# RetNet and quick-GELU on one core: v of steps 0 to 5 and q of step 3 loaded through GpSimd's DMA queue instead of SP's

## The chip, the cores and the metric

The kernel runs on one core of one Trainium2 chip. A core has five engines that work side by side, each through its own list of instructions in order: TensorE (PE) multiplies matrices, and its weight loads are counted apart (PEld); VectorE (DVE) and ScalarE (ACT) do elementwise work; GpSimd (POOL) does some of that and issues DMAs; SyncE (SP) issues DMAs alone. All DMAs, whoever issues them, are carried by the same 16 DMA engines. DMAs that SP or ACT issue appear in the profile as "hardware_dynamic" queues, those of GpSimd as "software_dynamic".

The metric is the device time of one execution in microseconds. An instruction waits for others by semaphores; a wait holds up everything behind it on the same engine, and that holds for DMA issues too.

## The reference: what is computed

Two blocks follow each other. The first is the RetNet recurrence for 4 batches, 8 heads, 768 positions and a head size of 64:

```python
gamma = 1.0 - 2.0 ** (-5.0 - np.arange(H))
for t in range(S):
    state = gamma * state + einsum('bhd,bhe->bhde', k[:, :, t], v[:, :, t])
    y[:, :, t] = scale * einsum('bhd,bhde->bhe', q[:, :, t], state)
```

Its output, regrouped to 3072 tokens of 512 numbers, goes through a feed-forward block with weights `w_in` (512 x 2048) and `w_out` (2048 x 512):

```python
h = x @ w_in
g = h * (1.0 / (1.0 + np.exp(-1.702 * h)))
return g @ w_out
```

The two weights arrive as 64-bit floats and are narrowed to 32 bits on the core.

## The kernel before

The recurrence is done in chunks of 64 positions. A step j handles one chunk of two batches; there are 24 steps, four steps make a block of 512 tokens, and six blocks go through the feed-forward part. While the first two blocks are computed, the kernel must also load and narrow the weights. This first stage, some 145 us, is written out by hand as one long list of names in the function's text (lines 998 to 1014): each engine carries out its own share of the list in that order, and so does each DMA queue.

The names that matter here, with j a step:

- `q{j}`, `k{j}`, `v{j}`: load the chunk of q, k or v (`load`, lines 131 to 170). For steps 0 to 5, q and k take four DMAs each and v two, all through `plain` and line 146, in pieces of 256 bytes; each of the three is 256 KB. q goes through SP; k through ACT for step 0 and through GpSimd for steps 1 to 5; v through SP. Buffers: q and v have two each, so v{j} has to wait until step j-2 has used its v, and q{j} until q{j-2} has been turned.
- `w{n}a`, `w{n}b`: fetch one half of a pair of weight columns, 512 KB (`fetch`, line 186), through SP, into one of three raw buffers; w3 needs the buffer that w0 leaves.
- `abs{n}` (ScalarE, L212), `half{n}` (VectorE, L216 to L218), `rest{n}` (VectorE, L222 to L227): narrow a weight. For w0 the two halves are done apart (0a, 0b).
- `turn{j}` (TensorE, L255): transpose k and then q of step j; `turned{j}` (ScalarE, L266) copies the results out of PSUM.
- `step{j}` (TensorE, L294): scores of q and k; `masked{j}` (VectorE, L323) masks them. `step-{j}` (L302, L311, L317): the products that read v and the masked scores; `step5-4` is step 5's scores followed by step 4's products. `updated{j}` (VectorE, L371, L373), `state{j}` (L330) and `x{j}` (L352) take their results, `aged{j}` (ScalarE, L362) scales the state by `whole`, and `decay{j}` (ScalarE, L277) scales k.
- `causal` (GpSimd, L919): cuts the mask, once VectorE has made it (`mask`, L954). `whole` (GpSimd, L930): loads a small table. `late` users of GpSimd in this stage are L940 to L948 (`anew`).
- `up0.h.n` (TensorE, L417): products of the feed-forward block 0 with weight n, each with a `gate` (ScalarE, L398).

One more order is imposed by the framework. Each kind of DMA queue has eight completion semaphores that its DMAs take in turn, SP and ACT sharing one set of eight, GpSimd having another. A DMA is issued only when the DMA eight places before it, which used the same semaphore, has landed.

Of the kernel before, what the change touches and what calls it, by code (L numbers as in the profile page):

```python
# [28 lines left out]
def kernel(  # L29
# [29 lines left out]
    pe, act, dve, pool, sp = nc.tensor, nc.scalar, nc.vector, nc.gpsimd, nc.sync  # L59
# [68 lines left out]
    NEW = 6  # L128
    QKV = {}

    def load(j, what="qkv"):

        b, c = j // NC * 2, j % NC
        rows = slice(c * D, (c + 1) * D)
        keep = tc.keep_in_program_order if j < 2 * CB else lambda i: i

        def plain(name, src, tag, bufs, engine=sp):
            t = two.tile([P, H, D], F32, name=name + "_in", tag=tag, bufs=bufs)  # L140
            QKV[name, j] = t
            for i in range(2):
                if j < NEW:
                    to, at = t[i * D:(i + 1) * D], src[b + i, :, rows, :].rearrange("h p d -> p h d")
                    for n in range(1 if name == "v" else 2):
                        keep(engine.dma_start(*((to, at) if name == "v" else (to[:, n:H:2], at[:, n * HP:(n + 1) * HP]))))  # L146
                else:
                    for r in range(2):
                        keep(engine.dma_start(t[r * D:(r + 1) * D, i * HP:(i + 1) * HP],
                                              src[b + i, r * HP:(r + 1) * HP, rows, :].rearrange("h p d -> p h d")))  # L150

        if j < NEW:
            if "q" in what:
                plain("q", q, "q_sq", 2)
            if "k" in what:
                plain("kn", k, "k_sq" if j in (0, 1, 4, 5) else "o", 2, pool if j else act)
        elif "q" in what:
            for name, src in (("q", q), ("k", k)):
                t = two.tile([P, H, D // C4, C4], F32, name=name + "_sq")
                for r0 in range(0, P, C4):  # L160
                    for n in range(D // C4):
                        t0 = c * D + n * C4
                        tc.keep_in_program_order((pool if (name, j) == ("k", 2 * CB - 1) else sp).dma_start(
                            t[r0:r0 + C4, :, n], src[b + r0 // D, :, t0:t0 + C4, r0 % D:r0 % D + C4]
                            .rearrange("h p d -> p h d")))
                QKV[name, j] = t
        if "v" in what:
            if j >= NEW and c < NC - 1:
                plain("kn", k, "kn", 1)
            plain("v", v, "v", 2)  # L170


    w1v = moe_w_in.bitcast(U32).rearrange("(c p) (f two) -> p c f two", p=P, two=2)
# [72 lines left out]
    def turn(j):  # L246

        QT[j], KT[j] = home(j, "qT"), home(j, "kT")
        if j < NEW:

            x = QKV.pop(("q", j)), QKV["kn", j]
            TURNED[j] = p = [ps.tile([P, HP, P], F32, name="pt", tag="y") for i in range(2)]
            for n in (1, 0) if j else (0, 1):
                for s in range(HP):
                    pe.matmul(p[n][:, s, :], x[n][:, 2 * s:2 * s + 2].rearrange("p r d -> p (r d)"), ident, is_transpose=True)  # L255
        else:
            for t, name in ((QT[j], "q"), (KT[j], "k")):
                tc.keep_in_program_order(dve.transpose(
                    t.rearrange("p h t -> p (h t)"), QKV.pop((name, j)).rearrange("p h n d -> p (h n d)")))
        if 2 * CB <= j < NCH - 2:  # L260
            load(j + 2, "qk")
# [113 lines left out]
    def step(j, f=None):  # L375
        attend(j, f)
        if j is not None:
            masked(j)
            if j > 2 * CB:
                decay(j)  # L380
        if f is not None:
            c = f % NC
            if c == 0:
                updated(f)
            else:
                by_state(f)
            output(f)
            if 0 < c < NC - 1:
                aged(f)
                updated(f)  # L390
        if j is not None and 2 * CB < j < NCH - 1:
            load(j + 1, "v")
# [541 lines left out]
    def late_loads():  # L934
        load(2 * CB, "qkv")
        load(2 * CB + 1, "qk")
# [174 lines left out]
```

## Time and profile before

| | us |
|---|---|
| median of 3 runs | 657.14 (656.97 to 660.35) |
| the profiled execution | 657.92 |
| its span | 656.2 |
| TensorE busy in the span | 638.8 (97%) |
| VectorE, GpSimd, ScalarE busy | 437.0, 188.4, 166.4 |
| TensorE busy in the first 60 us | 46.2 |
| data moved by DMA in the first 60 us | 203 GB/s on average |

The profile is one execution; its 657.92 us are 1.7 us more than its span, which runs from the first to the last instruction. Times given in the text as "at 8.47" are us from the start of that span. In a timeline each line has the start, the length, the engine, the line of the kernel, the operation, and out<-in with the count; a bracket at its end tells how long the engine had been idle before, and what ended that. A length beside a DMA issue is the time of issuing, not of the transfer; the trace tells apart when a transfer lands, engine by engine.

In the first 60 us TensorE is idle for 13.8 us, in the rest of the span for 3.6 us.

### The profile page before, as it was taken

What the parts mean: (1) busy time and instruction counts of PE and PEld (TensorE: products, weight loads), DVE (VectorE), ACT (ScalarE), POOL (GpSimd) and SP (SyncE); (2) the same over time, 40 slices, a digit from 0 to 9 for tenths busy, and PEclk for the clock granted to TensorE, in tenths of its full rate; (3) what the DMA queues carried; (4) which work ended last, traced back from release to release, by engine and by line L of the source; (5) the groups of instructions that cost most, each with busy time, mean ns of one, the idle gap of its engine ahead of it and who ended that gap; (6) DMA issues with size and microseconds to landing.
All of it is one profiled execution on the core that took longest, in us unless ns stands there. A gap on an engine that the chain in (4) does not pass through costs nothing.

```text
span 656.2 us, 15176 instructions
## 1 busy us (share of the span) xinstructions
PE 638.8 (97%) x6390; PEld 577.5 (88%) x6390; DVE 437.0 (67%) x609; ACT 166.4 (25%) x320; POOL 188.4 (29%) x218
## 2 busy tenths in 40 slices
PE   7689999999999999999999999999999999999997
PEld 3678888888888888889999888999888999888997
DVE  3789989999936963348885246987145986144854
ACT  4664234551000000333100323110333110332210
POOL 6400341310478218000627200535300334300000
PEclk9799999999999999999999999999999999999999
DMA  9995567853233455541577821477931254501142
GB/s 178 208 247 187 141 138 218 221 120 61 50 93 148 117 155 149 193 137 41 156 163 212 244 33 49 116 191 180 262 59 49 78 158 144 204 15 49 57 153 98
DMA packets 146229, 89.77 MB, mean 137 GB/s; under 512 B 129552, under 2 KB 132368, under 8 KB 145136
## 3 DMA queue, kind: packets, MB, share of 16 engines
q1 hardware_dynamic: 133680, 44.40, 29.8%
q0 software_dynamic: 9712, 38.43, 19.0%
q10 hardware_dynamic: 2768, 5.96, 2.6%
q8 instruction: 50, 0.82, 0.5%
q14 instruction: 19, 0.16, 0.1%
HBM read 71.32 MB, written 14.94 MB: 131 GB/s over the span
## 4 chain that ended last, share of the span: by engine, by line
PE 94%; DMA 2%; DVE 2%; SPq 1%; issue 0%; ACT 0%
PE pq L717 27%; PE px L590 17%; PE pd L852 15%; PE pz L590 8%; PE ph L417 8%; PE ph L488 6%; PE py L590 4%; PE pa L294 2%; DMA W<-in_moe_w_in_dram 2%; PE pa L302 2%; PE py L317 2%; PE py L311 2%; SPq L146 1%; PE pb L488 1%; PE pt L255 0%; DVE W L218 0%
## 5 line engine op out<-in xcount | busy, mean ns | idle before, releaser
L692 POOL DMA_DIRECT2D LATE<-W2D x28 | 15.5, 553 | 245.2 <-PE pq L717 123.8
L717 PE MATMUL pq<-W,G 128*128 128x128 f32 x672 | 80.2, 276 | 0.0
L717 PEld LDWEIGHTS pq<-W,G 128*128 128x128 f32 x672 | 77.6, 192 | 0.6
L590 PE MATMUL px<-X,W1A 128*128 128x256 f32 x256 | 60.5, 379 | 0.0
L590 PE MATMUL px<-X,LATE 128*128 128x256 f32 x256 | 60.5, 379 | 0.0
L717 PE MATMUL pq<-LATE 128*128 128x128 f32 x448 | 59.8, 276 | 0.0
L417 PE MATMUL ph<-X,W1A 128*128 128x256 f32 x256 | 57.4, 382 | 2.0 <-DVE X L352 1.1
L417 PEld LDWEIGHTS ph<-X,W1A 128*128 128x128 f32 x256 | 48.0, 190 | 9.0 <-DVE X L352 1.2
L717 PEld LDWEIGHTS pq<-LATE 128*128 128x128 f32 x448 | 54.5, 192 | 0.4
L590 PEld LDWEIGHTS px<-X,LATE 128*128 128x128 f32 x256 | 48.6, 190 | 6.6
L590 PEld LDWEIGHTS px<-X,W1A 128*128 128x128 f32 x256 | 48.4, 190 | 6.5
L852 PE MATMUL pd<-W,G 128*128 128x256 f32 x224 | 49.6, 381 | 0.0
L852 PEld LDWEIGHTS pd<-W,G 128*128 128x128 f32 x224 | 42.2, 190 | 5.9
L398 ACT ACTIVATE G<-G 128x512 f32<-128x512 f32 x49 | 30.8, 629 | 45.2 <-DVE G L645 19.7
L635 DVE TENSOR_TENSOR G<-pz,vv 128x512 f32<-128x512 f32 x16 | 11.1, 691 | 46.7 <-ACT vv L605 46.6
L852 PE MATMUL pd<-W,LATE 128*128 128x256 f32 x160 | 35.2, 380 | 0.0
L852 PEld LDWEIGHTS pd<-W,LATE 128*128 128x128 f32 x160 | 30.2, 190 | 4.3 <-DVE LATE L574 0.2
L739 ACT ACTIVATE o<-pq 128x512 f32<-128x512 f32 (+1 forms) x14 | 7.6, 544 | 90.7 <-PE pq L717 90.7
L590 PE MATMUL pz<-X,W1A 128*128 128x256 f32 x128 | 30.3, 379 | 0.0
L590 PE MATMUL py<-X,W1A 128*128 128x256 f32 x128 | 30.2, 379 | 0.0
L590 PE MATMUL pz<-X,LATE 128*128 128x256 f32 x128 | 30.2, 379 | 0.0
L717 PE MATMUL pq<-LATE,G 128*128 128x128 f32 x224 | 29.6, 275 | 0.0
(211 smaller groups left out, 1175.9 us busy)
## 6 DMA issues: line engine op xcount, KB each, us to landing
LATE<-W2D POOLq DMA_DIRECT2D x28, 768.0 KB, 4.9
W<-in_moe_w_in_dram SPq DMA_DIRECT2D x12, 512.0 KB, 5.9
W<-in_moe_w_out_dram SPq DMA_DIRECT2D x10, 512.0 KB, 6.1
out_dram<-o POOLq DMA_DIRECT2D x20, 256.0 KB, 4.0
q_sq<-in_q_dram SPq DMA_DIRECT2D x144, 32.0 KB, 2.2
v_in<-in_v_dram SPq DMA_DIRECT2D x72, 64.0 KB, 2.6
LATE<-W1D ACTq DMA_DIRECT2D x3, 1536.0 KB, 7.4
LATE<-W1D POOLq DMA_DIRECT2D x3, 1536.0 KB, 8.1
```

Source lines behind the costliest of these rows:

```text
L294: pe.matmul(pa[HALF[w], u, 0, s, :], kt[HALF[u], w, s, :], qt[HALF[u], w, s, :], start=True, stop=True)
L302: pe.matmul(pa[HALF[u], w, 1, s, :], kd[HALF[w], HP * u + s, :], vn[HALF[w], HP * u + s, :], start=True, stop=True)
L311: pe.matmul(py[HALF[o], u, 1, 2 * w + s2, :], old[HALF[u], w, 2 * s2 + o, :], qt[HALF[u], w, 2 * s2 + o, :], start=True, stop=True)
L317: pe.matmul(py[HALF[o], w, 0, 2 * u + s2 if f < NEW else 2 * s2 + u, :], vn[HALF[w], HP * u + s, :], a[HALF[w], u, s, :], start=True, stop ...
L398: pin(act.activation(g, h[:, i], AF.Gelu_apprx_sigmoid))
L417: pe.matmul(h[:, ab], w, X[:, 2 * th + c // 2, c % 2, :], start=(ab == 0 and c == 0), stop=(c == 3), skip_group_check=True)
L488: pe.matmul(acc[:, u, :], w, x, start=(start and u == 0 and c == 0), stop=(stop and c == 1), skip_group_check=True)
L590: pe.matmul(acc[:, u, :], w1(2 * d + u, sw)[:, c, :], X[:, sx, c, :], start=(start and u == 0 and c == 0), stop=(stop and c == 1), skip_gr ...
L635: dve.tensor_add(a[3], z, v)
L692: engine.dma_start(c, W2D[i])
L717: pe.matmul(p0[:, j, :], a[:, d], w[:, d], start=(new and j == 0 and d == 0), stop=(d == NP // 2 - 1), skip_group_check=True)
L852: pe.matmul(p0[:, n, :], g1(m, p, sa)[:, n * P:(n + 1) * P], W2[:, sb, p, :], start=(new and p == 0 and n == 0), stop=(last and p == NP - ...
```

## The change

`plain`, which issues the DMAs of one tile, takes the engine as an argument. The change passes GpSimd for v of steps 0 to 5 and for q of step 3:

```diff
         if j < NEW:
             if "q" in what:
-                plain("q", q, "q_sq", 2)
+                plain("q", q, "q_sq", 2, pool if j == 3 else sp)
             if "k" in what:
                 plain("kn", k, "k_sq" if j in (0, 1, 4, 5) else "o", 2, pool if j else act)
...
         if "v" in what:
             if j >= NEW and c < NC - 1:
                 plain("kn", k, "kn", 1)
-            plain("v", v, "v", 2)
+            plain("v", v, "v", 2, pool if j < NEW else sp)
```

The list of names stays as it is. TensorE, VectorE and ScalarE have the same instructions in the same order. On GpSimd the order in this stage becomes: small tables, k1, v0, k2, `causal`, v1, `whole`, k3, v2, q3, k4, v3, k5, v5, v4, then L940 and what follows. On SP it becomes: q0, w0b, q1, w0a, q2, w2b, w2a, q4, w3b, w3a, q5, w1b, w1a, w5b, w5a, w6. Sixteen DMAs change their queue, and with them the DMA eight places ahead for which each DMA waits.

## The prediction

> **What bounds the kernel now.** I read the page first, then the busy times by stage, the chain of waits, and the timelines of the queues and engines over the first 60 us.
>
> ```profile
> PE 638.8 (97%) x6390; PEld 577.5 (88%) x6390; DVE 437.0 (67%) x609; ACT 166.4 (25%) x320; POOL 188.4 (29%) x218
> ```
>
> TensorE sets the time: 656.2 - 638.8 = 17.4 us of the span is not TensorE work. By stage:
>
> ```profile
> 10.00:20.00 10.00, 6.72 (x107) 4.10 (x106) 6.67 (x11) 7.54 (x25) 6.52 (x10) 0.97 1.22 205
> 20.00:30.00 10.00, 7.79 (x176) 7.06 (x177) 7.22 (x12) 6.21 (x17) 4.25 (x7) 0.69 1.19 208
> 30.00:40.00 10.00, 9.34 (x168) 8.05 (x167) 7.25 (x10) 6.58 (x20) 0.00 (x0) 1.00 0.95 207
> 40.00:50.00 10.00, 7.78 (x130) 6.66 (x128) 9.79 (x13) 7.57 (x22) 0.00 (x0) 1.00 1.12 280
> ```
>
> The first figure after the length is TensorE's busy time, the last three are its granted clock, the DMA share and GB/s. 3.3, 2.2, 0.7 and 2.2 us of idle lie in these four rows, and from 60 us on TensorE is full. So this change, which ends before 50 us, can move only the first stage, and what it moves there is kept to the end. In that stage the DMA engines are full (shares near or over 1), which matters more than who issues. The chain of waits goes through them at w0a and again at w1:
>
> ```profile
> 8.47 9.20 DMA W<-in_moe_w_in_dram
> ...
> 36.45 4.00 DMA W<-in_moe_w_in_dram
> ```
>
> The SP queue, start and length of each group of issues:
>
> ```profile
> 7.13 1.30 SPq L146 DMA_DIRECT2D v_in<-in_v_dram  x2
> 8.47 1.08 SPq L186 DMA_DIRECT2D W<-in_moe_w_in_dram  x1
> 9.83 1.78 SPq L146 DMA_DIRECT2D v_in<-in_v_dram  x2
> 11.74 4.80 SPq L146 DMA_DIRECT2D q_in<-in_q_dram  x4
> 16.58 1.48 SPq L186 DMA_DIRECT2D G<-in_moe_w_in_dram  x2
> 18.17 1.95 SPq L146 DMA_DIRECT2D v_in<-in_v_dram  x2
> 20.16 9.04 SPq L146 DMA_DIRECT2D q_in<-in_q_dram  x8
> 29.30 1.96 SPq L186 DMA_DIRECT2D W<-in_moe_w_in_dram  x2
> ```
>
> These are v0, w0a, v1, q2, w2, v2, q3 with q4, w3. An undisturbed issue takes some 0.62 us; the long groups are SP held up. The weights w3 leave only behind q3 and q4. Then ScalarE, VectorE and GpSimd:
>
> ```profile
> 37.84 1.14 ACT L212 ACTIVATE W1A<-W 128x1024 f32<-128x1024 f32 x1 [3.42 <-DMA W<-in_moe_w_in_dram]
> ```
> ```profile
> 39.02 0.69 DVE L216 TENSOR_SCALAR W1A<-W1A 128x1024 f32<-128x1024 f32 x1 [2.35 <-ACT W1A L212]
> ...
> 47.13 0.68 DVE L216 TENSOR_SCALAR W1A<-W1A 128x1024 f32<-128x1024 f32 x1
> ```
> ```profile
> 12.82 1.84 POOL L919 TENSOR_SCALAR_AFFINE_SELECT mask<-mask 64x512 f32<-64x512 f32 x2 [4.08 <-DVE mask L954]
> 14.62 1.08 POOL L930 DMA_DIRECT2D whole<-in_col_decay_dram  x2
> ...
> 50.84 1.02 POOL L943 COPY cold<-cold 64x4 f32<-64x4 f32 x1 [24.12 <-ACT G L277]
> ```
>
> abs3 waits for w3 (3.42 us) and VectorE loses 2.35 us. GpSimd stands on a mask until 12.82 and is free from 26.7 to 50.8.
>
> **The change, part by part.** Sixteen DMAs (12 of v, 4 of q3) leave SP: 16 x 0.62 = 9.9 us of its issue time. The same sixteen come to GpSimd. Its k issues take 0.62 to 0.66 us, its shortest (row decay) 0.55, its longest (L467) 1.28; a v DMA has twice the pieces of a k DMA but nearest is k, so 0.67, and 16 x 0.67 = 10.7 us (8.8 to 20.5). The 24.1 us that GpSimd waits before L943 hide this; after it the last v leaves near 45, so 5 us of that cover stay, and if they went, the wait before L942 (16.2 us) would hide the rest. No instruction of PE, VectorE or ScalarE is added. What counts is when transfers land.
>
> *Price of a transfer.* In three rows the queues moved 205, 208 and 207 GB/s. Call the q, k or v of a step a tile (0.262 MB, 1.27 us at 207) and a half of w a block (0.524 MB, 2.53 us). Transfers of both queues land nearly in the order of issue: a 1 KB load (L930) issued at 15.15 took 5.3 us behind the others. From w0a's landing at 17.67, eight tiles and four blocks give 17.67 + 10.2 + 10.1 = 38.0 for w3; it landed at 37.76. A tile on GpSimd's queue may cost less (4 KB packets at 322 ns against sixteen of 29 ns: 0.87 of 1.27) or more (below): 0.9 to 1.8, and I take 1.27, which fits a mixed stage.
>
> *w0a, a gain.* It is issued at 7.13 instead of 8.47, and k2 (now behind v0 on GpSimd) falls behind it: it lands 1.27 us earlier, at 16.4. updated0 and step1 follow it: step1 at 19.85 instead of 21.13.
>
> *v1 and whole, a loss.* On GpSimd v1 stands behind the mask: 14.66 instead of 9.83. Without v, SP issues q2 and w2 from 8.6 to 12.5 (before, 11.74 to 18.1). So v1 lands behind k2, q2 and w2: 16.4 + 2.5 + 5.1 + 1.3 = 25.3 (18.7 before). step-1, which reads it, started at 24.09: +1.2 us, all of w0a's gain and as much again. whole, now behind v1, lands at 25.4 (20.4); aged1 (21.02) and turned2 (24.8) move to 25.4 and 27.8, in step with that.
>
> *q3, a loss.* Every DMA waits for the one eight before it on its kind of queue. v2 waits so for v1 (25), q3 for whole: q3 leaves at 26.0 to 28.5 instead of 20.16 to 25.5. SP meanwhile issues q4 (22.8, when turn2 is done) and w3 (25.4, 29.30 before). In order of landing: k3 26.5, q4 27.8, v2 29.1, w3 34.1, q3 35.4. turn3 read q3 at 32.42; it ends at 36.05 instead of 33.05: +3.0. step3 and masked3 follow through updated2 at +2.3.
>
> *w3, a gain that q3 eats.* w3 lands at 34.1 and abs3 no longer waits; the 2.35 us before half3 are gone. But masked3 stands ahead of half3 on VectorE and ends at 38.9: half3 starts at 38.95 against 39.02. Net -0.1.
>
> *q5 and w1, the next late thing.* q5 waits on SP for turn3 (36.05, before 33.20), and w1, w5 are queued behind it: w1 is issued at 38.7 and 39.3 (36.45, 37.89). After q3 come k4, v3, k5, q5, v5 and two blocks: 35.4 + 6.35 + 5.06 = 46.8 for w1 (42.43). abs1 then ends at 48.0 and half1, at 47.13 before, starts 0.9 late. rest1 and masked4 stand behind it on VectorE, and step5-4 on TensorE waits for masked4: +0.9.
>
> *The slowest engine.* A landing counts when the last of 16 DMA engines has finished. In the trace's landing records the last came 1.49 us after the fifteenth for w0a and 1.40 for w3a, while GpSimd's queue was active or just drained, and 0.01 for w1a. Now that queue is active until w1: I add 1.5 for w1, with 0 and 1.9 (w3b) as ends. The Trainium skill, DMA: Bandwidth & Descriptors, section Latency and other measured facts, says DMA engines 7 and 15 are usually slower, with fetches of GpSimd's descriptors as a best guess. The trace agrees on one late engine; it does not name it. If the guess held and each piece counted, the lag would double with the pieces; by the opposite reading it would be 0, and the sum 1.5 less.
>
> *v3, v4, v5, k4, k5.* k4 and k5 (needed at 39.4 and 43.4) and v3 (needed at 40.4) land at 36.7, 40.5 (its issue waits eight places, for q3) and 38.0: hidden by 2.4 us at the least; cover gone, each costs its lateness on TensorE. v4's buffer comes free with step-3 as before, and it has some 4 us until step5-4.
>
> Sum: w0a, v1, q3 and w3 together -0.1 at half3; w1 +0.9; slowest engine +1.5; step5-4's shift, +2.3. The clock was half from 19.4 to 26.3; a TensorE waiting until 25.3 may keep it so for one more 3.4 us window, 0 to 1.7 us; most lies under q3's wait, so I add 0.6. In all +2.9: 657.92 would become 660.8, and the median 657.14 becomes **660.0 us**.
>
> **The rivals.**
>
> *Faster: GpSimd's transfers need not queue behind the blocks.* For: k4's first part, issued at 18.13, landed at 25.86, before w2a (17.69, 26.77); a packet of 4 KB is cheaper. Against: L930's 5.3 us. If v1 takes 5.5 us it lands at 20.8, turn2 ends first (22.8), step-1 gains 1.3; q3 lands by 31, w3's 2.35 us are kept for the most part: -1.3 - 1.8 = -3.1, 654.0 us. It decides when v1 lands before 22.8 and q3 before 32.
>
> *A wash.* If the rate stays at 207 and one engine does not lag, w1's 0.9 and the clock are all that is left, or nothing where w3's gain is bigger: 657 us, -1.5 to +1.5. The Trainium skill, same page, section Issuing engines are not separate DMA queues, says that issuing from several engines saves only the sequencer's issue time. By that rule alone, with SP's issue off the end's path, this is the outcome; the rows above say that order of landing changes as well.
>
> *Slower by much.* The clock: v1 later than 25 leaves TensorE idle in the window to 26.3, then half-rate to 29.7 or 33.1. up0.0.0 (3.6 us at full rate) doubles and q3's lateness no longer covers it: +1.7 to 3.4 on my sum, 663 us.
>
> **How the numbers follow.** Forecast (+1 to +5): 0.42; faster rival (-1.5 to -4.5): 0.23; wash: 0.18; slow rival (+5 to +9): 0.17. 0.5% is 3.3 us, about what a measurement of this kernel can tell from no change: 653.9 and 660.4 are the bounds. Faster by over that: 0.16, of the faster rival. Slower: all of the slow rival and half of the forecast, 0.38. Within: 0.46. The range leaves out 0.1 at each end: 653.6 (w0a's, w3's gains whole) to 665.0 (bounds of lag and clock together). The forecast's own range is 658 to 662.
>
> **What would show it.** step1 near 19.9 (w0a right); step-1 near 25 with a wait on v_in; turn3 waiting for q_in near 35; no wait of abs3 on W; abs1 waiting for W near 46; TensorE idle before step5-4; a granted clock under 0.69 in 20 to 30. Wrong if v1 lands before 23, if q3 lands before 32, or if the 30 to 40 row moves well above 207 GB/s.

## The result and the profile after

The changed kernel takes 658.94 us (median of 22 executions, 657.67 to 662.96) against 656.96 us before: a ratio of 1.0028 with a 95% interval of 1.0017 to 1.0039, or +1.8 us (1.1 to 2.6; the two medians differ by 2.0). That is slower, by less than the 0.5% that a measurement was said to tell from no change. The forecast was 660.0 us, +2.9 us.

One thing has to be known before the traces are read. The profiled execution of the changed kernel (657.67 us) is the fastest of its 22, and that of the kernel before (657.92 us) lies 1 us above its own median. The two traces therefore differ by -0.25 us where the medians differ by +2.0, and they cannot show where the loss comes from. So both kernels were traced a second time (below: "second trace", 658.49 us after and 658.20 us before).

First the page's busy times, and the stages of the changed kernel from 10 to 50 us: after the length come the busy times of TensorE, its weight loads, VectorE, ScalarE and GpSimd, then TensorE's granted clock (the share of its full speed that it was allowed), the DMA share and GB/s.

```profile
PE 639.3 (97%) x6390; PEld 577.3 (88%) x6390; DVE 436.8 (67%) x609; ACT 166.5 (25%) x320; POOL 199.9 (30%) x234
```
```profile
10.00:20.00 10.00, 7.17 (x143) 4.45 (x143) 7.56 (x13) 8.04 (x25) 7.60 (x11) 1.00 1.13 248
20.00:30.00 10.00, 6.98 (x142) 5.76 (x141) 7.03 (x11) 6.31 (x20) 6.47 (x10) 0.71 0.91 210
30.00:40.00 10.00, 9.33 (x161) 7.92 (x161) 7.84 (x10) 5.88 (x17) 5.20 (x8) 0.94 0.71 152
40.00:50.00 10.00, 9.85 (x142) 8.59 (x141) 9.25 (x13) 8.36 (x25) 2.06 (x4) 1.00 1.05 312
```

GpSimd has 16 instructions and 11.5 us more; the busy times of the other engines differ by 0.5 us at most. Between 30 and 40 us the DMA share falls from 0.95 to 0.71, and from 207 to 152 GB/s. The second traces say the same (share 0.98 before, 0.79 after): with the change the DMA engines run out of issued work there. Part of the lower share has another reason. The moved tiles travel in packets of 4 KB, which took 292 and 314 ns on average in the two traces after, where the sixteen packets of 256 bytes that they replace took 28 to 29 ns each before. Over the first 60 us the same 203 to 204 GB/s need a DMA share of 0.83 and 0.87, against 0.95 and 0.96 before; the packets make 0.07 to 0.08 of that difference, an estimate from 448 and 7168 of them. The faster rival had named this in its favour, but the freed share was not turned into time.

The queues show why issued work runs out. SyncE, and then GpSimd, in the first trace after:

```profile
7.14 0.60 SPq L186 DMA_DIRECT2D W<-in_moe_w_in_dram  x1
7.96 3.00 SPq L146 DMA_DIRECT2D q_in<-in_q_dram  x4
11.00 1.13 SPq L186 DMA_DIRECT2D G<-in_moe_w_in_dram  x2
20.72 2.91 SPq L146 DMA_DIRECT2D q_in<-in_q_dram  x4
23.67 1.11 SPq L186 DMA_DIRECT2D W<-in_moe_w_in_dram  x2
34.49 3.08 SPq L146 DMA_DIRECT2D q_in<-in_q_dram  x4
37.61 1.13 SPq L186 DMA_DIRECT2D W<-in_moe_w_in_dram  x2
```
```profile
14.49 1.38 POOL L146 DMA_DIRECT2D v_in<-in_v_dram  x2
15.86 1.28 POOL L930 DMA_DIRECT2D whole<-in_col_decay_dram  x2
17.13 2.48 POOL L146 DMA_DIRECT2D kn_in<-in_k_dram  x4
22.49 0.69 POOL L146 DMA_DIRECT2D v_in<-in_v_dram  x1 [2.88 <-DMA v_in<-in_v_dram]
23.41 0.68 POOL L146 DMA_DIRECT2D v_in<-in_v_dram  x1 [0.23 <-DMA G<-in_moe_w_in_dram]
24.09 2.45 POOL L146 DMA_DIRECT2D q_in<-in_q_dram  x4
```

SP (w0a, q2, w2, q4, w3, q5, w1) now stands empty from 12.1 to 20.7 us, where q4 waits for turn2 to free its buffer, and from 24.8 to 34.5 us, where q5 waits for turn3. GpSimd issues v1 at 14.49, behind the mask, and v2 only after 2.88 us of waiting for v1's landing, the DMA eight places ahead of it; in the second trace it waits 4.72 us. q3 stands behind v2.

The waits on TensorE, in the second trace after (step1, step-1, up0.0.0, turn3, step5-4):

```profile
20.47 0.95 PE L294 MATMUL pa<-G 64*64 64x64 f32 x32 [3.17 <-DVE state L371]
...
24.40 1.55 PE L302 MATMUL pa<-v_in,G 64*64 64x64 f32 x30 [1.08 <-DMA v_in<-in_v_dram]
...
29.25 3.72 PE L417 MATMUL ph<-X,W1A 128*128 128x256 f32 x16 [0.79 <-DVE X L352]
...
35.56 0.63 PE L255 MATMUL pt<-UB,q_in 128*128 128x128 f32 x4 [2.15 <-DMA q_in<-in_q_dram]
...
54.72 0.69 PE L294 MATMUL pa<-G 64*64 64x64 f32 x32 [1.19 <-ACT W1A L212]
```

and the same places in the second trace before (step-1 without a wait):

```profile
20.74 0.69 PE L294 MATMUL pa<-G 64*64 64x64 f32 x32 [3.44 <-DVE state L371]
...
22.80 1.13 PE L302 MATMUL pa<-v_in,G 64*64 64x64 f32 x32
...
31.70 0.63 PE L255 MATMUL pt<-UB,q_in 128*128 128x128 f32 x4 [0.45 <-DMA q_in<-in_q_dram]
...
52.26 0.69 PE L294 MATMUL pa<-G 64*64 64x64 f32 x32 [0.91 <-DVE G L323]
```

Two waits for DMAs, on v1 (1.08 us) and on q3 (2.15 us), are there as forecast. From one second trace to the other step-1 comes later by 1.6 us, turn3's q part by 3.9 us and step5-4 by 2.5 us. The bracket of step5-4 after names L212, the abs of w5; but in all four traces step5-4 starts 0.15 us after masked4 has ended, and before the change that was ahead of the end of this abs. So it is masked4 that releases it. In the chain of waits of the first trace after, v1 and the last quarter of q3 have taken the place of w0a and w1:

```profile
14.49 7.45 DMA v_in<-in_v_dram
...
25.93 7.67 DMA q_in<-in_q_dram
```

### The profile page after: what moved, and what is told of

It is laid out like the page before. It is cut to its first block, busy times and chain, and to the rows that moved or that the text cites. A ratio compares the mean times of both kernels' runs of the same rounds, so it can differ in the third digit from the quotient of the medians.

```text
span 655.9 us, 15180 instructions
## 1 busy us (share of the span) xinstructions
PE 639.3 (97%) x6390; PEld 577.3 (88%) x6390; DVE 436.8 (67%) x609; ACT 166.5 (25%) x320; POOL 199.9 (30%) x234
## 4 chain that ended last, share of the span: by engine, by line
PE 93%; DMA 3%; POOL 1%; DVE 1%; issue 1%; ACT 0%; POOLq 0%
PE pq L717 27%; PE px L590 17%; PE pd L852 15%; PE pz L590 8%; PE ph L417 8%; PE ph L488 6%; PE py L590 4%; PE pa L294 2%; DMA v_in<-in_v_dram 2%; PE py L317 2%; PE py L311 1%; PE pa L302 1%; DMA q_in<-in_q_dram 1%; PE pb L488 1%; POOL kn_in L146 0%
## 5 line engine op out<-in xcount | busy, mean ns | idle before, releaser
L417 PE MATMUL ph<-X,W1A 128*128 128x256 f32 x256 | 59.4, 391 | 0.1
L417 PEld LDWEIGHTS ph<-X,W1A 128*128 128x128 f32 x256 | 49.4, 195 | 7.7 <-DVE W1A L227 0.4
L852 PEld LDWEIGHTS pd<-W,G 128*128 128x128 f32 x224 | 42.2, 190 | 5.9
L635 DVE TENSOR_TENSOR G<-pz,vv 128x512 f32<-128x512 f32 x16 | 11.1, 692 | 46.6 <-ACT vv L605 46.6
L717 PE MATMUL pq<-W,LATE 128*128 128x128 f32 x224 | 29.7, 275 | 0.5 <-issue 0.5
```

The costliest lines, as they stand in the source:

```text
L417: pe.matmul(h[:, ab], w, X[:, 2 * th + c // 2, c % 2, :], start=(ab == 0 and c == 0), stop=(c == 3), skip_group_check=True)
L635: dve.tensor_add(a[3], z, v)
L717: pe.matmul(p0[:, j, :], a[:, d], w[:, d], start=(new and j == 0 and d == 0), stop=(d == NP // 2 - 1), skip_group_check=True)
L852: pe.matmul(p0[:, n, :], g1(m, p, sa)[:, n * P:(n + 1) * P], W2[:, sb, p, :], start=(new and p == 0 and n == 0), stop=(last and p == NP - ...
```

## One gate: the start of half3

What a delay in this stage is worth can be read from VectorE. half3 waits for two things: abs3, which needs w3, and masked3, which stands ahead of it on VectorE and needs step3 on TensorE, so q3 and all that TensorE has to do before. In the first trace after it is masked3 (VectorE's timeline: masked3, half3, half1):

```profile
36.81 0.69 DVE L323 TENSOR_TENSOR G<-pa,mask 128x512 f32<-128x512 f32 x1
37.42 0.82 DVE L216 TENSOR_SCALAR W1A<-W1A 128x1024 f32<-128x1024 f32 x1
...
46.29 0.69 DVE L216 TENSOR_SCALAR W1A<-W1A 128x1024 f32<-128x1024 f32 x1 [0.55 <-ACT W1A L212]
```

The prediction showed the same place before: half3 at 39.02, 2.35 us idle for abs3. The second traces have masked3 and half3 so, first before, then after:

```profile
35.89 0.69 DVE L323 TENSOR_TENSOR G<-pa,mask 128x512 f32<-128x512 f32 x1 [0.30 <-PE pa L294]
37.09 0.69 DVE L216 TENSOR_SCALAR W1A<-W1A 128x1024 f32<-128x1024 f32 x1 [0.51 <-ACT W1A L212]
```
```profile
38.54 0.69 DVE L323 TENSOR_TENSOR G<-pa,mask 128x512 f32<-128x512 f32 x1
39.15 0.81 DVE L216 TENSOR_SCALAR W1A<-W1A 128x1024 f32<-128x1024 f32 x1
```

So before the change half3 waits for abs3, by 2.35 or 0.51 us, and after it no longer does. From half3 on, VectorE has its fixed work up to masked4, and TensorE waits for that. In every trace of this study but one, step5-4 starts 15.16 to 15.57 us after half3 (17.59 where SP issues everything, where more is late), and another 602.0 to 604.2 us follow. So half3's start carries a lateness of masked3 or of w3 to the end, and only the later of the two counts. Each ratio is taken against executions of the kernel before that were made beside it:

| kernel | ratio to before (95%) | w3 lands (last engine) | masked3 ends | abs3 ends | half3 starts | step5-4 after half3 |
|---|---|---|---|---|---|---|
| before, two traces | | 37.76; 35.83 | 36.67; 36.58 | 38.98; 37.06 | 39.02; 37.09 | 15.16; 15.17 |
| after, two traces | 1.0028 (1.0017 to 1.0039) | 34.36; 36.68 | 37.50; 39.23 | 36.15; 37.94 | 37.42; 39.15 | 15.55; 15.57 |
| all v, q3 on SP | 1.0026 (1.0013 to 1.0039) | 36.43 | 39.69 | 38.44 | 39.60 | 15.36 |
| q3 alone | 1.0011 (0.9998 to 1.0024) | 37.18 | 35.74 | 38.41 | 38.45 | 15.16 |
| change, v1 on SP | 1.0015 (1.0001 to 1.0030) | 35.58 | 35.17 | 36.79 | 36.82 | 15.16 |
| change, v1 ahead of mask | 1.0003 (0.9989 to 1.0018) | 37.13 | 37.30 | 38.37 | 38.41 | 15.34 |
| change, w1 ahead of q5 | 1.0052 (1.0033 to 1.0070) | 36.47 | 41.98 | 39.27 | 41.90 | 15.35 |
| both reorderings | 1.0036 (1.0015 to 1.0057) | 37.23 | 39.94 | 38.46 | 39.86 | 15.41 |
| v0 alone | 0.9995 (0.9983 to 1.0006) | 37.81 | 37.04 | 39.04 | 39.07 | 15.17 |
| v1 alone | 0.9997 (0.9984 to 1.0010) | 35.79 | 36.51 | 37.02 | 37.06 | 15.16 |
| all v, v1 ahead of mask, q3 on SP | 1.0051 (1.0031 to 1.0071) | 39.78 | 35.63 | 40.98 | 41.02 | 15.35 |
| k on SP too | 1.0090 (1.0070 to 1.0110) | 39.04 | 35.94 | 40.24 | 40.27 | 17.59 |

half3 starts within 0.1 us of the later of masked3's and abs3's ends in all 14 traces. Leaving out the last row, half3 ranges over 5.1 us, and what follows it to the end over 2.2 us (617.2 to 619.4). That second spread is larger than the 1.8 us in question, so the gate tells what the first stage costs in an execution, not all of its time. The gate was found with the traces in hand, so it is a reading that fits all of them, not a forecast that was tried. A single trace is one execution: half3 alone came at 39.02 and at 37.09 in the kernel before, so a row's half3 need not stand for its median (the trace with v1 on SP is of an execution 1.7 us under that kernel's median).

masked3 can be late without q3. With all v moved and q3 on SP, q3 had landed at 27.75, and masked3 still ended at 39.69: step-1 had waited for v1, and TensorE's clock was 0.5 from 20.8 to 34.4. The clock also lies on this path in the two traces with w1 ahead of q5, at 0.5 from 35.3 to 42.2 and from 35.0 to 38.4, between q3's landing and masked3.

## The experiments

Theory A was that the order of landing decides: v1 and whole late, q3 and w1 after them, with w0a's gain on the other side. Theory B was that each tile on GpSimd's queue has a price of its own, at the slowest of the DMA engines. Theory C was TensorE's lowered clock.

**The v alone, with q3 back on SP** (the edit as seen from the changed kernel).

```diff
-                plain("q", q, "q_sq", 2, pool if j == 3 else sp)
+                plain("q", q, "q_sq", 2)
```

> v of steps 0 to 5 through GpSimd, q3 back on SP. Theory A (order of landing: v1 and the whole table behind w2, q3 behind v1 by the eight-places rule, w1 behind q5): q3 leaves SP near 20 and lands near 26, so turn3 does not wait for it; v1 stays late. Expected 1 to 2 us less than the changed kernel, that is -0.2 to +0.8 us against before. Theory B (each tile on GpSimd's queue costs the slowest DMA engine more, whatever its place): six of seven tiles are still moved, so 6/7 of the loss of 1.9 us, +1.6 us.

Measured: 658.69 us, ratio 1.0026, as slow as the whole change. By ratio q3's move adds nothing that can be told once v has moved. In its trace whole lands by 25.8 us, step-1 waits 1.6 us for v_in, and up0.0.0 runs for 6.0 us, 3.7 in the second traces above, at a clock of 0.5. A expected most of the loss to go, and missed; B's +1.6 us fits this run.

**q3 alone** (seen from the kernel before).

```diff
-                plain("q", q, "q_sq", 2)
+                plain("q", q, "q_sq", 2, pool if j == 3 else sp)
```

> Only q3 through GpSimd, all v on SP. Theory A: with no v on GpSimd's queue q3 does not wait for v1 and whole; it leaves near 20 as before, and SP issues q4 and w3 earlier by up to 2.5 us; abs3's wait for w3 (3.42 us before) shrinks. Expected -0.5 to -1.5 us against before. Theory B: one of seven tiles, +0.3 us.

Measured: 657.84 us, 1.0011 (0.9998 to 1.0024). Here q3 comes early (26.2 to 28.5) and TensorE does not wait for it at all, but w3 lands at 37.18, and half3 stands until 38.45. abs3 in ScalarE's timeline of this kernel:

```profile
37.26 1.15 ACT L212 ACTIVATE W1A<-W 128x1024 f32<-128x1024 f32 x1 [3.72 <-DMA W<-in_moe_w_in_dram]
```

An earlier q3 is worth nothing while w3 is the later of the two. A's gain of 0.5 to 1.5 us did not come; B's +0.3 us lies inside the interval (-0.1 to +1.6 us).

**The change with v1 back on SP.**

```diff
-            plain("v", v, "v", 2, pool if j < NEW else sp)
+            plain("v", v, "v", 2, pool if j < NEW and j != 1 else sp)
```

> The change with v1 alone back on SP, where it stands between w0a and q2. Theory A: v1 lands near 18 ahead of q2 and w2, whole near 21; step-1 follows turn2 at once and starts some 1 us earlier than in the changed kernel, aged1 2 us earlier; q3 leaves GpSimd about 2 us earlier. Expected 1.5 to 2.5 us less than the changed kernel, -0.6 to +0.4 us against before. Theory B: +1.6 us against before.

Measured: 657.96 us, 1.0015 (1.0001 to 1.0030), between the two theories. v1 lands at 18.09, whole at 20.35 and q3 by 31.42, as A expected, but in time the interval (0.1 to 2.0 us) excludes neither A's +0.4 nor B's +1.6 us.

**The change with v1 named ahead of the mask.** "v1" moves in the list from behind "decay0" to behind "k2"; all sixteen DMAs stay on GpSimd.

```diff
-        k0 table q0 warm turn0 w0b rows warm k1 abs0b q1 turned0 step0 v0 w0a half0b mask k2 turn1 causal rest0b
-        masked0 decay0 v1 decay1 abs0a half0a step-0 updated0 turned1 q2 step1 rowd whole w2b turn2 w2a x0 k3
+        k0 table q0 warm turn0 w0b rows warm k1 abs0b q1 turned0 step0 v0 w0a half0b mask k2 v1 turn1 causal rest0b
+        masked0 decay0 decay1 abs0a half0a step-0 updated0 turned1 q2 step1 rowd whole w2b turn2 w2a x0 k3
```

> The change with v1 named before causal in the list, so that GpSimd issues it right after k2 (near 11 instead of 14.5) and not behind the mask. Theory A: v1 lands near 20, with or before w2, step-1 waits less by 1 us or more; whole stays late. Expected 0.5 to 1.5 us less than the changed kernel, +0.4 to +1.4 us against before. Theory B: the same as the changed kernel, +1.9 us.

Measured: 657.20 us, 1.0003 (0.9989 to 1.0018). v1 is issued at 11.1 us and lands by 21.0, step-1 starts at 23.22 without a wait (TensorE's timeline below), and whole lands 0.7 to 2.4 us earlier than in the two traces of the change. Sixteen DMAs on GpSimd thus cost +0.2 us in this order and +1.8 us in the other, and the two intervals overlap by no more than 0.0001: B falls, and the loss of the change is one of order.

```profile
22.24 1.06 PE L255 MATMUL pt<-UB,q_in 128*128 128x128 f32 x4
23.22 1.13 PE L302 MATMUL pa<-v_in,G 64*64 64x64 f32 x32
...
33.63 0.63 PE L255 MATMUL pt<-UB,q_in 128*128 128x128 f32 x4 [1.56 <-DMA q_in<-in_q_dram]
```

turn3 still waits 1.56 us for q3, and half3 waits for abs3 again, so this order does not mend everything. v1, whole, v2 and q3 all leave earlier with it; which of them brings back how much is not separated.

**The two kernels again, for a second trace.**

> The changed kernel once more, for a second trace of it: the first trace (657.67 us) is of the fastest of its 22 executions and can't show where the median's +2 us come from. If the order of landing is the cause (A), v1's second DMA lands after 23 us again with waits on v_in inside step-1, and a wait on DMA of over 0.5 us stands at turn3 or at step5-4; the start of step4 on TensorE, 51.11 in the first trace, comes at 52.5 or later in an execution near the median. If each tile on GpSimd's queue has a price of its own (B), the landings of v1, v2 and q3 stay where they were and the lateness is spread over all transfers up to w6.

> The kernel before once more, for a second trace of it: its first trace was about 1 us above its own median. Step4 on TensorE, 52.58 us in that trace, is expected between 50.5 and 52.0 for an execution near the median under either theory; v1 lands before 20 and step-1 starts without a wait on v_in.

Measured: 658.49 and 658.20 us. The second trace after looks as A expected: v1 at 24.89, turn3 waits 2.15 us, step4 at 52.83. That of before has step4 at 50.66, as expected. It is ahead of its first trace by 2 us at 52 us (step5-4 at 52.26 against 54.18), and loses this later: 1.56 of its 150 us from 300 to 450 are idle on TensorE, put down to "issue", where the first trace has none.

**w1 named ahead of q5, alone and with v1 ahead of the mask.**

```diff
-        w3a up0.0.0 masked2 turn3 k4 step-2 v3 q5 rest2 k5 gate0.0.0 turned3 updated2 state2 step3 up0.0.2
-        masked3 abs3 half3 x2 rest3 turn4 w1b step-3 aged3 gate0.0.2 turned4 state3 w1a w5b updated3 v5 decay4
+        w3a up0.0.0 masked2 turn3 k4 step-2 v3 w1b w1a q5 rest2 k5 gate0.0.0 turned3 updated2 state2 step3 up0.0.2
+        masked3 abs3 half3 x2 rest3 turn4 step-3 aged3 gate0.0.2 turned4 state3 w5b updated3 v5 decay4
```

> The change, with w1 named ahead of q5, so that SP issues it at about 34.5 us and not behind q5 at 37.6. If the order of landing decides (A), w1 lands 2 to 3 us earlier, abs1 no longer waits for it, the 1.17 us before step5-4 go, and q5, now later by 1.2 us, still comes before turn5: 0.5 to 1.2 us better than the change, +0.8 to +1.5 us against before. If each tile on GpSimd's queue has its price (B), w1's place changes nothing: +1.9 us as the change.

> The change with both repairs of order: v1 ahead of the mask on GpSimd, and w1 ahead of q5 on SP. By A the two add: +0.3 us (v1 ahead of the mask) less 0.5 to 1.2 gives -0.9 to -0.2 us against before. By B no better than v1 ahead of the mask alone: +0.3 us or more.

Measured: 660.88 us (1.0052) and 660.64 us (1.0036): worse than without. The first goes against both theories, the second against A alone, for B had named +0.3 us or more. The expectations took for granted that w1 would leave at 34.5. Its buffer was free, and without q5 ahead of it SP issued it straight behind w3 (four DMAs in the second line below), into the same stretch in which q3 was on its way. SP's timeline of the first of the two, then turn3's q part in TensorE's:

```profile
22.37 2.59 SPq L146 DMA_DIRECT2D q_in<-in_q_dram  x4
25.00 2.26 SPq L186 DMA_DIRECT2D W<-in_moe_w_in_dram  x4
37.63 2.59 SPq L146 DMA_DIRECT2D q_in<-in_q_dram  x4
```
```profile
36.51 1.09 PE L255 MATMUL pt<-UB,q_in 128*128 128x128 f32 x4 [3.38 <-DMA q_in<-in_q_dram]
```

q3 landed at 36.27 and half3 started at 41.90, 0.95 and 2.75 us later than in the second trace after. The other 1.8 us come from the clock: it was 0.5 from 35.3 on, and the way from turn3's q part to masked3 took 4.78 us instead of 2.98. In the other kernel's trace the clock costs 1.4 us in the same place. q3's own delay is about 1 us in both (34.62 against 33.39 with v1 ahead of the mask alone), so it explains only a part of the loss in these traces, and how much of the medians' loss it explains stays open. In the change, q5's wait for turn3 had kept w1 from being issued beside q3.

**v0 alone, and v1 alone** (argument of `plain` in the kernel before).

```diff
-            plain("v", v, "v", 2)
+            plain("v", v, "v", 2, pool if j == 0 else sp)
```
```diff
-            plain("v", v, "v", 2)
+            plain("v", v, "v", 2, pool if j == 1 else sp)
```

> Only v0 is issued by GpSimd. If the order of landing decides (A), this keeps the gain alone: w0a leaves SP 1.3 us earlier, step1 starts about 1 us earlier and v1, q2 and w2 follow 1.3 us earlier: -1.2 to 0 us against before. If each tile on GpSimd's queue has a price (B), a sixteenth of the change twice: +0.2 us.

> Only v1 is issued by GpSimd, behind the mask. By A this is the loss alone: v1 lands near 23 to 25 us and step-1 waits for it, with w0a where it was: +1.2 to +2.2 us against before. By B two of sixteen DMAs: +0.2 us.

Measured: 657.39 us (0.9995, interval 0.9983 to 1.0006) and 657.25 us (0.9997, 0.9984 to 1.0010). A's loss with v1 is not there. A gain with v0 can't be told: its interval, -1.1 to +0.4 us, holds most of A's range, and B's +0.2 us lies in both intervals. With v0 moved, w0a is issued at 7.12 as forecast but lands at 17.33, where the kernel before had 17.67 and 17.56: issued 1.35 us earlier, it took longer to land. The traces scatter, though. In the nine with v0 on GpSimd w0a landed at 15.29 to 17.92, 16.9 on average, and in the four with v0 on SP and k as before at 17.15 to 17.67, 17.5 on average. So some 0.5 us of the earlier issue arrive, not all of it. With v1 moved, v1 lands at 23.53, 4.8 us later than before, and that is just in time for TensorE, whose timeline shows turn2 and step-1 without a gap (below). In this execution the clock was 0.5 from 19.4 to 26.2, so turn2 took about twice as long as at full clock; at full clock step-1 would have had some 1 us to wait (an estimate: step1 and turn2 took 1.7 us together at full clock in the first trace after, 3.0 here).

```profile
21.55 1.11 PE L255 MATMUL pt<-UB,kn_in 128*128 128x128 f32 x4
22.46 1.06 PE L255 MATMUL pt<-UB,q_in 128*128 128x128 f32 x4
23.45 1.14 PE L302 MATMUL pa<-v_in,G 64*64 64x64 f32 x30
```

**All v on GpSimd, v1 ahead of the mask, q3 on SP.** The two diffs above on the change, q3's and v1's.

> All six v on GpSimd with v1 ahead of the mask, and q3 back on SP. The trace with v1 ahead of the mask but q3 on GpSimd showed TensorE waiting 1.56 us for q3; by A this goes and the gain of w0a stays: -1.2 to +0.2 us against before. By B twelve of sixteen DMAs, +1.5 us. If q3's place makes no difference where v1 comes early, +0.3 us as with q3 on GpSimd.

Measured: 661.15 us, 1.0051 (1.0031 to 1.0071), 3.2 us worse by ratio than the same kernel with q3 on GpSimd, and outside all three expectations: against A, and against B too, since fewer DMAs are on GpSimd. The wait for q3 is gone (it landed by 27.3), but the other side of the gate is late. abs3 in ScalarE's timeline of this kernel, then the product (L311) that waits for x2 behind half3 in TensorE's:

```profile
39.87 1.12 ACT L212 ACTIVATE W1A<-W 128x1024 f32<-128x1024 f32 x1 [6.63 <-DMA W<-in_moe_w_in_dram]
```
```profile
44.36 1.13 PE L311 MATMUL py<-G,state 64*64 64x64 f32 x32 [4.33 <-DVE X L352]
```

Without q3 in its queue GpSimd issued v3 at 26.15 and 27.28 (29.45 and 30.30 with q3 there) and k5 from 28.4 on (32.0). w3a, issued at 26.95 with v3, k5 and q5 in flight beside it, landed 12.8 us later, against 10.5 us there. The DMA share was 1.18 and 1.12 from 20 to 40 us: full engines, with transfers ahead that were needed later.

**The kernel before with k of steps 1 to 5 on SP too**, so that GpSimd's queue carries no tile.

```diff
-                plain("kn", k, "k_sq" if j in (0, 1, 4, 5) else "o", 2, pool if j else act)
+                plain("kn", k, "k_sq" if j in (0, 1, 4, 5) else "o", 2, sp if j else act)
```

> The kernel before with k of steps 1 to 5 issued by SP as well, so that GpSimd's queue carries no tile at all. Twenty more issues of 0.62 us stand on SP, 12 us, ahead of the weights, so the time rises by 1 to 6 us under either theory. What it is for is the slowest engine: if the lag of the last DMA engine behind the fifteenth (1.5 us for w0a and 1.4 to 1.9 for w3 in the trace before) comes from GpSimd's queue, it falls under 0.3 us at every block of weights; if it comes from full engines alone it stays at 0.5 to 2 us for some blocks.

Measured: 663.71 us, 1.0090, or +5.9 us, inside the expected 1 to 6. The lag of the last DMA engine behind the fifteenth, from the landing records, was 0.63 and 0.74 us for w0, 0.05 and 0.12 for w2, 0.02 and 2.05 for w3, 0.16 and 0.04 for w1. So a lag of 2 us can come without any tile on GpSimd's queue, while five of the eight blocks stay under 0.2 us. For w1a the lag was 0.01 and 0.38 in the two traces before, 0.43 and 0.27 with v0 or v1 alone moved, 1.11 and 0.31 after, 2.61 and 2.23 with w1 ahead of q5, but 0.03 in the change with v1 on SP, and 1.43 in the kernel with v1 ahead of the mask, which is no slower than before. It tends to be larger with more on GpSimd's queue; what makes an engine late stays open.

**Theory C** needs no run of its own, since each execution has a granted clock. Of the executions whose clock was 1.000 throughout, seven of the kernel before take 657.43 us on average and three of the changed kernel 659.81. Within kernels, over 223 executions, a mean clock lower by 0.001 goes with 0.1 us more (0.03 to 0.17); the mean clocks, 0.9955 before and 0.9947 after, differ by less than that. So a lower clock is not the cause of the loss. Where a lowered stretch falls is known for the traced executions alone, and there it can cost 1.4 to 1.8 us (w1 ahead of q5, above).

## Why the prediction was right, and where not

The direction and the range held, the change stayed within 0.5% as the forecast had it, and 660.0 us is 1.1 us high. The list of what would show it came out for the most part: the waits on v1, on q3 and on w1 are there, and abs3's wait is gone. But that the total came so near is in part luck, because errors of opposite sign cancel: the term at half3 was -0.1 us and came to some +1.4, w1 and the slowest engine were +2.4 and came to 0.4, and the clock was +0.6 and came to 0.1.

- **w0a, a gain.** Forecast at 16.4, it landed at 15.86 and 17.39 (step1 at 18.97 and 20.47; forecast 19.85). With v0 alone it gained 0.2 to 0.3 us for 1.35 us of earlier issue, and over the traces 0.5 us on average. The step failed in taking the landing to follow the issue one for one; what was queued ahead is the likely reason, and no run shows it by itself.
- **v1 and whole, a loss.** The mechanism was right: v1 behind k2, q2 and w2, at 23.13 and 24.89 (25.3 forecast), with a wait of step-1 on v_in. Its price was not a term of its own: v1 moved alone costs nothing that can be told. It costs together with the other v, and moving v1 ahead of the mask brings back 1.6 of the 1.8 us.
- **q3, a loss.** Right nearly to the figure in the second trace: landing 35.32 (35.4 forecast), but 33.59 in the first. The wait for v1 eight places ahead of v2 is in GpSimd's timeline of both. turn3's q part moved by 3.9 us between the second traces, +3.0 forecast.
- **w3, a gain that q3 eats.** Right, and the most useful step: abs3's wait is gone in both traces and half3 starts behind masked3, at 37.42 and 39.15 (38.95 forecast). But the -0.1 was taken against a half3 at 39.02, which was one execution's: at 37.09 in the second trace before, half3 waited only 0.51 us. The second traces make this term +2.1, the first -1.6; the medians leave about +1.4, an estimate: 1.8 less the 0.4 of the next point.
- **q5, w1 and the slowest engine.** w1 landed at 45.02 and 46.76 (46.8), and abs1 waits 1.20 and 1.21 us for it and ends at 46.26 and 48.00 (48.0). The two terms together were +2.4 at step5-4, and step5-4 came 0.4 us later after half3 (15.55 and 15.57 against 15.16). The lag's +1.5 is the term that was mis-sized: 0.1 to 1.1 us was measured for w1 after. Of w1's own lateness, half1 came 0.76 us later behind half3 than before, and at masked4 0.4 us of that were left.
- **The clock.** +0.6 was forecast, 0.1 us is what the executions give. In each of the two first traces 6.8 us run at 0.5, from 19.4 before and from 24.3 after. In 13 of the 14 traces the clock is lowered in this stage, in stretches of 3.4, 6.8 or 13.7 us that begin anywhere from 18.8 to 46.1. The Trainium skill, TensorE: Matmul & The Clock Gate, section What's actually happening, describes a free-running window of about 3.4 us; these lengths agree.
- **"A mixed stage at 207 GB/s".** It did not stay: 152 and 191 GB/s from 30 to 40 us, because both queues stood behind waits. The prediction had counted the waits of each DMA, not what they leave idle. That 4 KB packets are cheaper, which it named as a possibility, came out (292 and 314 ns against 464 for sixteen of 256 bytes).
- **GpSimd's time.** Right: 10.7 us of issue was forecast and 11.5 more busy time measured, and 4.78 us of the wait before L943 were left (5 forecast).

Of the rivals, "a wash" was nearest in size, but not for its reason: the same sixteen DMAs cost 0.2 or 1.8 us with one name elsewhere in the list. The Trainium skill, DMA: Bandwidth & Descriptors, section Issuing engines are not separate DMA queues, holds that issuing from several engines saves only issue time. That agrees with the absence of any gain here; the loss is one of order, which the move changes with it.

No version beats the kernel before: the best, v0 or v1 alone, are at 0.9995 and 0.9997, with 1 inside both intervals. What stays open is why v0's and v1's moves cost nothing that can be told singly and all v's together 1.7 us; the trace shows v2's wait for v1 on GpSimd and SP's empty stretches, but no run has all v moved with that wait taken away and q3 on time.

## What to carry to other kernels

Look for the instruction that joins the late chains (here half3, the later of w3's and q3's path) and measure every moved transfer against it; a transfer made earlier than that is worth nothing, and costs if it goes ahead of one that is needed there. A blocked queue is part of the schedule: q5's wait held w1 back, q3's place in GpSimd's queue held v3 back, and three of the four kernels without one of these brakes were 0.2 to 0.5% slower than with it (the fourth, all v moved with q3 on SP, was the same as the change). For an effect of 0.3%, trace both kernels more than once before dividing a difference into terms: two executions of one kernel had this gate 1.7 and 1.9 us apart.

## What was not expected of the hardware

- A landing follows its issue only in part when the engines are full (share 1.19 from 10 to 30 us with v0 alone moved): w0a, 1.35 us earlier out of SP, landed 0.2 to 0.3 us earlier there, and 0.5 us earlier on average over nine traces that scatter by 2.6 us.
- Two executions of the kernel before differ by 1.9 us at 52 us and agree to 0.3 us at the end: TensorE idles for up to 1.56 us between 300 and 450 us with no wait that the profile shows.
- With weights and tiles in flight together, the last of 16 DMA engines came up to 4.04 us behind the fifteenth (w2a with both reorderings; 3.98 us for w3a with w1 ahead of q5).
- The same 203 to 204 GB/s over the first 60 us took some 10% less of the DMA engines' time (share 0.83 and 0.87 instead of 0.95 and 0.96) with v and q3 on GpSimd's queue, in packets of 4 KB instead of 256 bytes.
